# One hand-set order for the end of each attention layer and the start of the Fourier layer behind it

## The chip, the cores and the metric

The kernel runs on one NeuronCore of a Trainium2 chip. The core has five engines that each work through a queue of their own, in order: TensorE (PE in the profile) for matrix products, VectorE (DVE), ScalarE (ACT), GpSimd (POOL), and SyncE (SP), which here only issues transfers. ACT issues some transfers as well. The metric is the device time of one execution in microseconds (us), the median over runs.

## The reference

Four layers work on x, 2048 rows of 640 numbers. Layers 0 and 2 are attention with a sliding, dilated window of 8 keys and 32 heads of 20; layers 1 and 3 are Fourier mixing, a product with a 2048x2048 matrix from the left and with a 640x640 matrix from the right. All is float32.

```python
def _A_ref(x, wqkv, wo):
    qkv = (x @ wqkv).reshape(B, S, 3, H, Dh)...
    idx = pos[:, None] - off[None, :]          # off = 0, 2, .., 14
    logits = jnp.einsum("bhsd,bhswd->bhsw", q, kg) * scale   # masked where idx < 0
    o = jnp.einsum("bhsw,bhswd->bhsd", _softmax(logits), vg)
    return o.reshape(B, S, D) @ wo

def _B_ref(x, dft_seq_re, dft_seq_im, dft_hid_re, dft_hid_im):
    a = jnp.einsum("bsd,ed->bse", x, dft_hid_re)
    b = jnp.einsum("bsd,ed->bse", x, dft_hid_im)
    return jnp.einsum("ts,bse->bte", dft_seq_re, a) - jnp.einsum("ts,bse->bte", dft_seq_im, b)

x = x + _A_ref(_layernorm(x), A_wqkv, A_wo)
x = x + _B_ref(_layernorm(x), B_dft_seq_re, B_dft_seq_im, B_dft_hid_re, B_dft_hid_im)
x = x + _A_ref(_layernorm(x), A_wqkv, A_wo)
x = x + _B_ref(_layernorm(x), B_dft_seq_re, B_dft_seq_im, B_dft_hid_re, B_dft_hid_im)
```

## The kernel before

**Numbers in two parts.** Every operand of a large product is kept as a high part (a rounded copy, made by ACT) and a low part (what is left, made by DVE or POOL with a subtraction). A product is three passes: high by high, high by low, low by high. To "split" a tile means to make both parts. Line numbers below are those of the kernel before.

**Attention layer** (`layer_a`, layers 0 and 2). The rows are handled in four chunks of 512, each of four tiles of 128 rows. The work is spread over numbered steps; a table `plan` holds for each step and each of some 35 phases the operations that fall there, and the lists in `CFG['ly']` set step and phase of nearly everything (`wo`: output products, `ln`: normalisations for the next layer, `t2`, `t3`: transpositions of the last chunks, `kvq`: which stores ACT issues instead of SP, and so on; many entries are half a step or a phase). The whole runs under a manual schedule: each engine gets its instructions in exactly the order in which they are written.

**Fourier layer** (`LayerB`, layers 1 and 3). Its first product, for a tile t of the sequence matrix, sums 16 blocks in five PSUM banks, m0, m1, xt, t0 and t1: `z_mm(s, p, t)` (L1114) is block s, 15 matmuls of 128x512 (five banks, three passes), or a third of it. The blocks of the first tile (t = 0) are already worked off inside the attention layer as its chunks get done. A block needs its row tile, normalised and split, and its piece of the matrix: loaded by `c_load` or `cw_load`, its high part made by `c_hi` on ACT (L1065), its low part by `c_lo` on DVE (L1097). In layer 0, `c_put` stores both parts to memory, from where layer 2 fetches them.

**The end of an attention layer**, behind the last step, stands in program text in a fixed order: last transposition (`pc_pe(67)`, L438, into bank pq; `pc_hi` L442 on ACT, `pc_lo` L459 on DVE), the last two output products (`wo_mm`, L636), and for each of the last two row tiles `wo_add` (L254 on DVE, stored by `wo_store`, L653), `wo_stats` (L259 to L268 on ACT), `wo_fin` (L276, only where the 1/sqrt is POOL's), `ln_tail` (L1051 on ACT for the high part, L1052 on DVE for a normalised copy) and `ln_lo` (L1039). Between them stand the splits of blocks 14 and 15 (layer 0 only) and `z_mm` 14 and 15. `z_late` are thirds of earlier blocks that are put off to the end: one in layer 2 (`z_late(68)`), none in layer 0.

**The start of the Fourier layer** (`run`). `evac(0)` copies the five banks out as high parts (`zt_put`: ACT, L1165) and low parts (DVE, L1167 and L1170) into tiles zo0, zo1, zo2 and ot; the banks are then free for the second tile, whose blocks s = 0 to 15 follow: `cw_load`, split, `z_mm(s, None, 1)`. Around them stand, in numbers set by `pre` and `post` in `CFG['run']`, the splits of the weights of the second product (`load_w`: transfers L297 into the two buffers called xa, ACT L225, DVE L227 and L229), sums of input tiles (`x_whole` L1243, `x_combine` L1253 to L1256), and, at the blocks listed in `y`, pieces of the first tile's second product (`ymm`, L1188, 12 matmuls each).

In `run` only PE is under the manual schedule. A scheduler that works with modelled times puts the instructions of the other engines in order, and may move those of `run` ahead, between the last operations of the attention layer:

```python
        def run(self, nstats):
            ...
            self.evac(0)
            ...
            with tc.manual_schedule(engines={nc.tensor.engine}):
                for s in range(NST):
                    ...
                    self.zpart(1, s, s + 1)
```

In `Stats`, `lno` decides for each chunk whether 1/sqrt(variance) is two ACT operations (logarithm and exponential) or a power on POOL; `lnv` decides for each row tile whether DVE or POOL makes its low part.

Of the kernel before, what the change touches and what calls it, by code (L numbers as in the profile page):

```python
# [55 lines left out]
 'wqg': [0, 0, 0, 0, 0, 1, 0, 1, 1, 1, 0, 1, 0, 1, 1, 0, 1, 0, 1, 0],  # L56
 'run': [{'pre': [0, 1, 0, 0, 2, 0, 0, 1, 0, 0, 0, 3, 0, 0, 0, 0],
          'post': [5, 1, 1, 2, 3, 4, 0, 5, 0, 7, 0, 3, 0, 4, 1, 5],
          'y': [[4, 4, 5, 6, 6], [9, 13, 14, 15, 16]]},
         {'pre': [6, 1, 0, 2, 3, 3, 0, 3, 0, 6, 0, 0, 2, 0, 0, 0],  # L60
          'post': [0, 0, 3, 2, 0, 4, 0, 0, 1, 0, 1, 0, 4, 0, 4, 3],
# [5 lines left out]
         'ord': [[2, 0, 1, 3, 4, 6, 5, 7], [2, 0, 1, 4, 6, 5, 3, 7], [0, 2, 1, 4, 3, 6, 5, 7]],  # L67
         'out': [20, 23, 27, 32, 36, 40, 44, 46],
         'wo': [22, 22, 26, 26, 29, 30, 33, 34, 39, 39, 42, 42, 45, 47, 49, 49],
# [5 lines left out]
         'z': [148, 149, 149, 151, 151, 156, 157, 157, 159, 159, 161, 162, 167, 168, 170, 171, 171, 173, 174, 175,  # L75
               175, 175, 176, 177, 179, 180, 180, 180, 181, 186, 186, 187, 188, 188, 188, 190, 191, 193, 194, 198,
# [4 lines left out]
         't2': [48, 48, 48, 48, 52, 52, 52, 52],  # L81
         't3': [57, 58, 60, 60],
         'wst': [0, 0, 0, 0, 0, 0, 0, -1, 0, 0, 0, 0, -1, 1, 0, 0],
         'kvq': [1, 0, 0, 1, 0, 0, 1, 0, 0, 0, 0, 0, 1, 0, 0, 0, 0, 0, 0, 0, 0, 0, 1, 0, 0, 0, 1, 0, 1, 0, 1, 0],
# [5 lines left out]
         'ph': ['evac dma peT0 pe hi fin peL z0 z1 red0 pe2 qk dma2 sA sB red1 sC av0 loE sD sE exp actl evacA sF '  # L90
                'evacO av1 qc dmaw dmac actL pe3w misc clo lnl dmas dmar pe3',
                'peT0 evac dma hi z0 peL red0 pe pe2 z1 fin qk dma2 sA av0 sD sE sB red1 loE sC evacA actL sF evacO '
                'exp dmac av1 actl qc misc clo dmas lnl dmar dmaw pe3 pe3w'],
# [3 lines left out]
         'lno': [True, False, False, True],  # L97
         'whole': [7, 57, 61],
         'lnv': [1, 1, 1, 0, 0, 1, 0, 0, 0, 1, 0, 0, 1, 1, 1, 1],
# [7 lines left out]
         'wo': [23, 23, 26, 27, 30, 31, 34, 35, 38, 38, 42, 42, 46, 47, 48, 49],  # L107
         'woph': 'z1',
         'ln': [41, 42, 42, 46, 53, 54, 55, 55],
# [3 lines left out]
         'z': [148, 150, 151, 151, 151, 152, 155, 156, 159, 160, 162, 169, 169, 170, 170, 170, 171, 171, 174, 174,  # L113
               175, 175, 177, 178, 178, 179, 179, 181, 182, 185, 186, 186, 186, 186, 187, 187, 188, 189, 192, 193,
               199, 205],
         'early': [5.3, 2.4, 6.1, 8.4, 5.9, 6, 7.3, 8.8, 7.4, 9.3, 13, 13.6, 9.3],
         'ym': [-7, 0],
         'ymph': 'pe2',
         't2': [49, 49, 48, 48, 50, 52, 52, 52],
         't3': [59, 58, 60, 60],  # L120
         'wst': [0, 0, 0, 1, 0, 0, 0, 0, 0, 0, 0, 0, 0, 0, 0, 0],
         'kvq': [1, 1, 1, 0, 0, 0, 0, 0, 0, 0, 0, 0, 0, 1, 0, 0, 1, 0, 0, 0, 0, 0, 1, 0, 0, 0, 0, 0, 0, 0, 1, 0],
# [4 lines left out]
         'zla': [0, 0, 2, 0, 0, 0, 1, 0, 1, 0, 0, 1, 0, 2],  # L127
         'ph': ['peT0 dma evac hi red0 pe z0 peL qk z1 fin sA pe2 red1 dma2 sB sD sC av0 loE sE clo evacA exp actl '
                'actL sF evacO av1 qc dmaw dmas misc pe3 lnl dmar dmac pe3w',
                'peT0 evac pe z0 dma red0 hi fin peL pe2 sA z1 qk dma2 sB red1 av0 sD loE evacA sC sE exp actL evacO '  # L130
                'sF av1 dmas dmaw actl qc misc dmar lnl pe3w clo dmac pe3'],
# [33 lines left out]
def tile_layers(ctx: ExitStack, tc: tile.TileContext, x, wqkv, wo, cs, cst, wre, wim, out):  # L165
# [178 lines left out]
    def layer_a(li, stats, handoff, prev):  # L344
# [623 lines left out]
        with tc.manual_schedule(engines=ENGINES):  # L968
# [8 lines left out]
            busy("pc_pe 67")  # L977
            pc_pe(67)
            pc_hi(67)
            pc_lo(67, True)  # L980
            busy("wo_mm 3 2 3")
            wo_mm(c, 2, None, 0, 2, 3)
            z_late(67)
            busy("wo_mm 3 3")
            wo_mm(c, 3, ("pq", "aux0"))
            z_late(68)
            wo_add(c, 2)
            wo_stats(c, 2)
# [5 lines left out]
            handoff.ln_tail(c, 2, xr, nstats)
            wo_add(c, 3)
            handoff.ln_lo(c, 2)
            busy("z_mm 14")
# [4 lines left out]
            if first:  # L1002
                handoff.c_hl(15)
                if CFG["cput"][15]:
                    handoff.c_put(15)
# [548 lines left out]
```

## Time and profile before

| | |
|---|---|
| median of 3 runs | 1750.72 us (1750.36 to 1752.07) |
| profiled execution | 1751.65 us, span of its instructions 1749.9 us |
| matmuls | 8828 |
| busy | PE 1720.2, DVE 1357.8, ACT 821.6, POOL 617.7 us |
| granted clock of TensorE, mean | 0.999 |
| transfers | 419.91 MB, mean 240 GB/s |

The page gives the busy time of each engine, groups of instructions and the chain of waits. The timeline lists an engine's instructions in order: start, duration, engine, line, operation, tiles, shapes, how many were merged, and in brackets how long the engine had been idle before and whose end it waited for. In the names of tiles numbers are left out: "m" is m0 or m1, "t" is t0 or t1, "s" is any of s0 to s3, "r" the large weight and input tiles. Matmuls overlap, so a matmul's duration is longer than the distance to the next one. Layer 0 ends at about 384 us, layer 1 at about 865, layer 2 at about 1249.

### The profile page before, as it was taken

The page shows a single profiled execution, that of the slowest core. Times are in us where ns is not written, and L with a number is a line of the kernel's source. Part 1 is how long each engine was busy: PE and PEld are TensorE (multiplying, and loading weights), DVE is VectorE, ACT ScalarE, POOL GpSimd, SP SyncE. Part 2 cuts the span into 40 slices and gives each one's busy share as a digit, 9 for nine tenths or more (in the row PEclk, how much of TensorE's full clock was granted, in tenths as well). Part 3 has the DMA queues.
Part 4 walks back from the last instruction along what each step waited for, and adds up shares of the span by engine and source line. Part 5 has one row for each costly group of instructions (what it writes and reads, how often), then busy time and mean ns, then how long its engine had stood idle before and what let it go on. Part 6 is the DMA issues. An engine that isn't in the chain of part 4 may idle for free.

```text
span 1749.9 us, 26561 instructions
## 1 busy us (share of the span) xinstructions
PE 1720.2 (98%) x8828; PEld 1497.1 (86%) x8828; DVE 1357.8 (78%) x2117; ACT 821.6 (47%) x1814; POOL 617.7 (35%) x572
## 2 busy tenths in 40 slices
PE   9999999999999999999999999999999999999999
PEld 6888888778888888888888889888788888888888
DVE  5999999878767767767639998899786677677673
ACT  5654644654445445445534434445443443443441
POOL 4899999940000000000019997899200000000000
PEclk9999999999999999999999999999999999999999
DMA  6786668968787687687557865788697867867861
GB/s 235 246 295 198 206 229 309 338 212 317 250 263 228 215 271 232 210 276 224 188 163 256 280 201 182 236 300 287 205 356 227 263 205 253 263 217 237 262 205 53
DMA packets 266713, 419.91 MB, mean 240 GB/s; under 512 B 22192, under 2 KB 144560, under 8 KB 266320
## 3 DMA queue, kind: packets, MB, share of 16 engines
q1 hardware_dynamic: 255088, 410.68, 71.1%
q10 hardware_dynamic: 11488, 7.54, 1.4%
q8 instruction: 70, 1.15, 0.3%
q14 instruction: 67, 0.55, 0.1%
HBM read 332.99 MB, written 85.14 MB: 239 GB/s over the span
## 4 chain that ended last, share of the span: by engine, by line
PE 81%; DVE 6%; DMA 4%; POOL 3%; ACT 3%; issue 2%; SPq 0%; ACTq 0%; DVEq 0%; POOLq 0%
PE m L473 16%; PE aux L1188 15%; PE m L1289 11%; PE t L1289 10%; PE aux L636 6%; PE pq L1289 5%; PE xt L1289 5%; PE t L1114 4%; PE m L1114 4%; PE xt L1114 2%; DVE pr L553 2%; DVE pr L596 1%; POOL pr L611 1%; DMA win<-cs_in 1%; POOL pr L556 1%
## 5 line engine op out<-in xcount | busy, mean ns | idle before, releaser
L473 PE MATMUL m<-r,s 128*128 128x512 f32 (+1 forms) x1920 | 429.3, 379 | 1.5 <-DVE r L755 0.9
L473 PEld LDWEIGHTS m<-r,s 128*128 128x128 f32 x1920 | 350.3, 188 | 57.5 <-DVE r L755 1.3
L1282 ACT CAST r<-win 128x512 fp32r<-128x512 f32 x242 | 147.1, 620 | 174.5 <-DVE win L1318 104.2
L1188 PE MATMUL aux<-r2a,zo 128*128 128x320 f32 x768 | 226.0, 309 | 0.0
L553 DVE TENSOR_TENSOR pr<-pq,win 128x1280 f32<-128x1280 f32 x128 | 189.8, 1483 | 37.8 <-PE aux L1188 20.3
L611 POOL TENSOR_TENSOR pr<-pr 128x640 f32<-128x640 f32 x126 | 207.6, 1648 | 26.3 <-DVE pr L596 25.2
L556 POOL TENSOR_TENSOR pr<-pr 128x640 f32<-128x640 f32 x125 | 179.5, 1436 | 88.8 <-DVE pr L553 88.7
L1188 PE MATMUL aux<-pr,zo 128*128 128x320 f32 x704 | 208.0, 309 | 0.0
L1283 DVE TENSOR_TENSOR r<-win,r 128x512 fp32r<-128x512 f32 x242 | 162.7, 687 | 41.4 <-ACT r L1282 39.0
L596 DVE TENSOR_TENSOR pr<-pq,win 128x1280 f32<-128x1280 f32 x128 | 190.3, 1488 | 2.5
L276 POOL TENSOR_TENSOR stats<-stats,mhalf 128x1 f32<-128x1 f32 (+1 forms) x27 | 19.6, 725 | 468.7 <-ACT stats L270 468.7
L1289 PE MATMUL m<-r,r 128*128 128x512 f32 x600 | 153.2, 390 | 0.8 <-DVE r L1283 0.7
L1188 PEld LDWEIGHTS aux<-r2a,zo 128*128 128x128 f32 x768 | 144.1, 188 | 2.1
L1188 PEld LDWEIGHTS aux<-pr,zo 128*128 128x128 f32 x704 | 132.2, 188 | 2.4
L1289 PEld LDWEIGHTS m<-r,r 128*128 128x128 f32 x600 | 112.3, 188 | 24.6 <-DVE r L1283 1.6
L1289 PE MATMUL t<-r,r 128*128 128x512 f32 x492 | 131.9, 390 | 0.0
L612 POOL TENSOR_TENSOR pr<-pr 128x320 f32<-128x320 f32 x126 | 113.5, 901 | 9.9
L566 DVE TENSOR_REDUCE lg<-pr 128x64 f32<-128x640 f32 (+1 forms) x128 | 105.8, 827 | 12.7 <-POOL pr L556 12.5
L1318 DVE TENSOR_TENSOR win<-win,win 128x512 f32<-128x512 f32 x109 | 75.0, 690 | 48.9 <-DMA win<-cs_in 47.6
L1114 PE MATMUL m<-s,r 128*128 128x512 f32 x348 | 107.3, 395 | 4.1 <-DVE zo L1167 1.3
L1289 PEld LDWEIGHTS t<-r,r 128*128 128x128 f32 x492 | 92.3, 188 | 19.8
L1114 PE MATMUL t<-s,r 128*128 128x512 f32 x348 | 106.5, 394 | 2.7 <-DVE ot L1170 2.3
(296 smaller groups left out, 3236.0 us busy)
## 6 DMA issues: line engine op xcount, KB each, us to landing
win<-cs_in SPq DMA_DIRECT2D x346, 256.0 KB, 4.2
r<-xc SPq DMA_DIRECT2D x240, 256.0 KB, 4.2
win<-kvb SPq DMA_DIRECT2D x96, 440.0 KB, 4.6
xa<-cs_in SPq DMA_DIRECT2D x120, 256.0 KB, 4.1
win<-kvb SPq DMA_DIRECT2D x64, 360.0 KB, 5.2
xc<-sg SPq DMA_DIRECT2D x28, 512.0 KB, 5.6
xr<-xs SPq DMA_DIRECT2D x40, 320.0 KB, 3.7
kvb<-stg SPq DMA_DIRECT2D x36, 320.0 KB, 2.6
```

The lines of the kernel that those rows point to most:

```text
L473: nc.tensor.matmul(mt[g][:, : GW[q]], st[:, a, k], wq[q][:, b, k], start=n == 0, stop=n == 14)
L553: nc.vector.tensor_tensor(pr, q, wview(u, jp, 0, [[1, FE]]), op=ALU.mult)
L556: nc.gpsimd.tensor_tensor(pv[:, :, 0:10], pv[:, :, 0:10], pv[:, :, 10:20], op=ALU.add)
L566: nc.vector.tensor_reduce(rows(lgs[u], jp), pv.rearrange("p (a h) d -> p a h d", h=HE), axis=AX.X, op=ALU.add,)
L596: nc.vector.tensor_tensor(pr.rearrange("p j w (h d) -> p (j w) h d", d=DH), rows(lgs[u], jp).unsqueeze(3).to_broadcast([P, 2 * W, HE, DH]) ...
L611: g.tensor_tensor(pr[:, :, 0:4], pr[:, :, 0:4], pr[:, :, 4:8], op=ALU.add)
L612: g.tensor_tensor(pr[:, :, 0:2], pr[:, :, 0:2], pr[:, :, 2:4], op=ALU.add)
L1114: self.last = nc.tensor.matmul(self.z[t][k], self.xn[c][:, a, j, k * P : (k + 1) * P], self.ct[s][:, b], start=s == 0 and i == 0, stop=s = ...
L1188: self.last = nc.tensor.matmul(self.ym[e][:, :320], zt[(k, a, ri)][:, j2 * P : (j2 + 1) * P], w[:, e * 320 : (e + 1) * 320], start=(k, a, ...
L1282: nc.scalar.copy(hi, raw)
L1283: nc.vector.tensor_tensor(lo, raw, hi.bitcast(F32), op=ALU.subtract)
L1289: nc.tensor.matmul(bank, w(a, kb), hl[b], start=start and (a, b) == (0, 0), stop=stop and (a, b) == (1, 0),)
```

## The change

The end of the attention layer becomes a list of small operations, one letter each, and `CFG['ly'][..]['tail']` gives the order of all of them, for layer 0 and for layer 2. The list now also holds the eviction of the first tile, piece by piece (`E`, `e0` to `e4`), the loads of the second tile's first three blocks (`G0` to `G2`) and the splits of its first two (`h0 k0 h1 k1`: high and low part), all under the manual schedule of every engine. `run` does those of the first three that the list leaves out, and everything that it schedules itself is issued behind the last instructions of the eviction on ACT and DVE. In layer 0, the splits and stores of blocks 14 and 15 (`c14 d14 p14 c15 d15 p15`) come first; in layer 2 the put-off third (`z68`) does.

```diff
+         'tail': 'c14 d14 p14 c15 d15 p15 P H L M2 z67 M3 z68 A2 S2 F2 T2 A3 l2 Z14 z69 S3 F3 T3 l3 G0 G1 G2 Z15 E '
+                 'e0 h0 k0 e1 e2 e3 e4 h1 k1'},
...
+         'tail': 'z68 P H L M2 z67 M3 A2 S2 F2 c14 d14 p14 T2 A3 l2 Z14 z69 S3 F3 c15 d15 p15 T3 l3 G0 G1 G2 Z15 E '
+                 'e0 h0 k0 e1 e2 e3 e4 h1 k1'}],
...
-            wo_add(c, 2)
-            wo_stats(c, 2)
-            wo_fin(c, 2, 3)
-            if first:
-                handoff.c_hl(14)
...
+            done = C["tail"].split()
+            assert all(t[0] in "Ghk" for t in set(tail) - set(done))
+            for t in done:
+                tail[t]()
+            h.done = set(done)
...
-            self.evac(0)
...
-            with tc.manual_schedule(engines={nc.tensor.engine}):
+            with ExitStack() as st:
+                for x in (self.last_a, self.last_v):
+                    st.enter_context(tc.issue_after(x.ins))
+                st.enter_context(tc.manual_schedule(engines={nc.tensor.engine}))
                 for s in range(NST):
...
-                    self.zpart(1, s, s + 1)
+                    for t, fn in (("G", lambda: self.cw_load(1, s)), ("h", lambda: self.c_hi(s, 1)), ("k", lambda: self.c_lo(s))):
+                        if f"{t}{s}" not in self.done:
+                            fn()
+                    self.z_mm(s, None, 1)
```

Around this many entries of the tables move by a half-step, a step or a phase; three to name:

```diff
-         'lno': [True, False, False, True],
+         'lno': [True, False, False, False],
...
-         'lnv': [1, 1, 1, 0, 0, 1, 0, 0, 0, 1, 0, 0, 1, 1, 1, 1],
+         'lnv': [1, 1, 1, 0, 0, 1, 0, 0, 0, 1, 0, 0, 1, 1, 0, 1],
...
-          'y': [[4, 4, 5, 6, 6], [9, 13, 14, 15, 16]]},
+          'y': [[3, 4, 5, 6, 8], [9, 13, 14, 14, 15]]},
```

In layer 0 the last chunk's 1/sqrt thus goes to POOL, and so does the low part of the tile before the last; and the pieces of the second product stand behind blocks 3, 4, 5, 6 and 8 instead of 4, 4, 5, 6 and 6.

ACT at the end of layer 0, before, from the last tile's statistics on (`s` at L1065 are splits of blocks, `r2a` and `pr` at L225 weights, `zo` at L1165 the eviction):

```order
L267 ACTIVATE stats_3928<-stats_3928,eps_65 128x1
L268 ACTIVATE stats_3928<-stats_3928 128x1
L1065 CAST s_660_4257<-win_4117 128x512
L284 ACTIVATE stats_3928<-stats_3928 128x1
L1051 ACTIVATE r_3_636_4047<-xa_4142,stats_3928 128x640
L225 ACTIVATE pr_675_4331<-xa_4332 128x640
L1065 CAST s_667_4303<-win_4301 128x512
L1065 CAST s_684_4356<-win_4354 128x512
L1165 CAST zo_662_4282<-m_496_3155 128x512
L1165 CAST zo_662_4282<-m_497_3156 128x256
```

And in the changed kernel (whose line numbers are a little higher: L1074 for L1065, L1060 for L1051, L1164 for L1165, L229 for L225):

```order
L274 ACTIVATE stats_3935<-stats_3935 128x1
L288 ACTIVATE stats_3935<-stats_3935 128x1
L1060 ACTIVATE r_3_637_4048<-xa_4143,stats_3935 128x640
L1164 CAST zo_666_4288<-m_496_3155 128x512
L1074 CAST s_670_4294<-win_4267 128x512
L1164 CAST zo_666_4288<-m_497_3156 128x256
L1164 CAST zo_667_4289<-m_497_3156 128x256
L1164 CAST zo_667_4289<-xt_3157 128x512
L1164 CAST zo_668_4290<-t_499_3158 128x512
L1164 CAST ot_4291<-t_500_3159 128x512
L1074 CAST s_671_4308<-win_4269 128x512
L229 ACTIVATE r2a_4334<-xa_4335 128x640
```

The split of block 15 is gone from between the statistics and the normalisation, and no weight and only block 0's split stands ahead of or within the eviction.

DVE at the same place, before, from block 15's low part on (L1243 is a sum of input tiles):

```order
L1097 TENSOR_TENSOR s_660_4257<-win_4117,s_660_4257 128x512
L1052 TENSOR_SCALAR win_4261<-xa_4142,stats_3928 128x640
L1243 TENSOR_TENSOR s_695_4432<-r_2_569_3615 128x1024
L1039 TENSOR_TENSOR r_3_636_4047<-win_4261,r_3_636_4047 128x640
L227 SCALAR_TENSOR_TENSOR pr_675_4331<-xa_4332,pr_675_4331 128x640
L1097 TENSOR_TENSOR s_667_4303<-win_4301,s_667_4303 128x512
L1097 TENSOR_TENSOR s_684_4356<-win_4354,s_684_4356 128x512
L1167 TENSOR_TENSOR zo_662_4282<-m_496_3155,zo_662_4282 128x512
L1170 TENSOR_TENSOR zo_663_4283<-m_497_3156,zo_662_4282 128x256
L1170 TENSOR_TENSOR zo_663_4283<-m_497_3156,zo_663_4283 128x256
L1167 TENSOR_TENSOR zo_664_4284<-xt_3157,zo_663_4283 128x512
L1243 TENSOR_TENSOR s_696_4434<-r_0_418_2649 128x1024
```

And in the changed kernel (L1106 for L1097, L1061 for L1052, L1245 for L1243, L1048 for L1039, L1166 and L1169 for L1167 and L1170):

```order
L1061 TENSOR_SCALAR win_4262<-xa_4143,stats_3935 128x640
L1048 TENSOR_TENSOR r_3_637_4048<-win_4262,r_3_637_4048 128x640
L1166 TENSOR_TENSOR zo_666_4288<-m_496_3155,zo_666_4288 128x512
L1106 TENSOR_TENSOR s_670_4294<-win_4267,s_670_4294 128x512
L1169 TENSOR_TENSOR zo_667_4289<-m_497_3156,zo_666_4288 128x256
L1169 TENSOR_TENSOR zo_667_4289<-m_497_3156,zo_667_4289 128x256
L1166 TENSOR_TENSOR zo_668_4290<-xt_3157,zo_667_4289 128x512
L1169 TENSOR_TENSOR zo_668_4290<-t_499_3158,zo_668_4290 128x256
L1169 TENSOR_TENSOR ot_4291<-t_499_3158,zo_668_4290 128x256
L1166 TENSOR_TENSOR ot_4291<-t_500_3159,ot_4291 128x512
L1245 TENSOR_TENSOR s_698_4447<-r_2_570_3616 128x1024
L1245 TENSOR_TENSOR s_699_4449<-r_0_419_2651 128x1024
```

Both sums have moved from within the eviction to behind it; block 1's low part follows them.

PE at the end of layer 2, before (aux with r2a are output products, pq the last transposition, m the banks of the first product):

```order
L636 MATMUL aux_1798_12507<-r2a_9372,zo_1787_12455 128x320 x9
L438 MATMUL pq_12517<-ident_69,zo_1749_12175 128x128 x4
L636 MATMUL aux_1797_12497<-r2a_9372,zo_1787_12455 128x320 x6
L636 MATMUL aux_1798_12507<-r2a_9372,zo_1787_12455 128x320 x6
L636 MATMUL pq_12538<-r2a_9372,zo_1789_12457 128x320 x15
L636 MATMUL aux_1801_12554<-r2a_9372,zo_1789_12457 128x320 x15
L1114 MATMUL m_1658_11591<-s_1774_12336,r_3_1779_12392 128x512
```

And in the changed kernel:

```order
L640 MATMUL aux_1798_12505<-r2a_9373,zo_1787_12453 128x320 x9
L1123 MATMUL m_1659_11591<-s_1774_12338,r_3_1779_12385 128x512
L1123 MATMUL m_1660_11592<-s_1774_12338,r_3_1779_12385 128x512
L1123 MATMUL xt_11593<-s_1774_12338,r_3_1779_12385 128x512
L1123 MATMUL t_1662_11594<-s_1774_12338,r_3_1779_12385 128x512
L1123 MATMUL t_1663_11595<-s_1774_12338,r_3_1779_12385 128x512
L442 MATMUL pq_12520<-ident_69,zo_1750_12176 128x128 x4
L640 MATMUL aux_1797_12495<-r2a_9373,zo_1787_12453 128x320 x6
L640 MATMUL aux_1798_12505<-r2a_9373,zo_1787_12453 128x320 x6
```

The five matmuls of the put-off third have moved from behind the output products to ahead of the transposition.

More of the change, by code (lines that the diff above doesn't have):

```diff
@@ L994, in layer_a @@
[L994 to L997, printed above, removed]
-            handoff.z_mm(14, None)
-            z_late(69)
-            wo_stats(c, 3)
-            wo_fin(c, 3, 4)
[L1002 to L1005, printed above, removed]
-            handoff.ln_tail(c, 3, xr, nstats)
-            handoff.ln_lo(c, 3)
-            busy("z_mm 15")
-            handoff.z_mm(15, None)
+            none = lambda *a: None
@@ new lines, in layer_a @@
+            h = handoff
+            tail = {
+                "P": lambda: (busy("pc_pe 67"), pc_pe(67)),
+                "H": lambda: pc_hi(67),
+                "L": lambda: pc_lo(67, True),
+                "M2": lambda: (busy("wo_mm 3 2 3"), wo_mm(c, 2, None, 0, 2, 3)),
+                "M3": lambda: (busy("wo_mm 3 3"), wo_mm(c, 3, ("pq", "aux0"))),
+                "E": lambda: h.zt_new(0),
+            }
+            for j in (2, 3):
+                s = 12 + j
+                tail |= {
+                    f"A{j}": lambda j=j: wo_add(c, j),
+                    f"S{j}": lambda j=j: wo_stats(c, j),
+                    f"F{j}": lambda j=j: wo_fin(c, j, j + 1),
+                    f"T{j}": lambda j=j: h.ln_tail(c, j, xr, nstats),
+                    f"l{j}": lambda j=j: h.ln_lo(c, j),
+                    f"c{s}": (lambda s=s: h.c_hi(s)) if first else none,
+                    f"d{s}": (lambda s=s: h.c_lo(s)) if first else none,
+                    f"p{s}": (lambda s=s: h.c_put(s)) if first and CFG["cput"][s] else none,
+                    f"Z{s}": lambda s=s: (busy(f"z_mm {s}"), h.z_mm(s, None)),
+                }
@@ new lines, in layer_a @@
+            for t in (67, 68, 69):
+                tail[f"z{t}"] = lambda t=t: z_late(t)
+            for s in range(3):
+                tail |= {
+                    f"G{s}": lambda s=s: h.cw_load(1, s),
+                    f"h{s}": lambda s=s: h.c_hi(s, 1),
+                    f"k{s}": lambda s=s: h.c_lo(s),
+                }
+            for k in range(KD):
+                tail[f"e{k}"] = lambda k=k: h.evac1(0, k)
+            done = C["tail"].split()
+            assert all(t[0] in "Ghk" for t in set(tail) - set(done))
```

90 lines of the change are left out of this document (36 added, 54 removed), and 16 rows, old and new, of the table CFG.

## The prediction

> **What bounds the kernel now.** I read the page first, then busy time in stretches of 50 us, then the timeline of each engine around the two places where an attention layer hands over to a Fourier layer.
>
> ```profile
> PE 1720.2 (98%) x8828; PEld 1497.1 (86%) x8828; DVE 1357.8 (78%) x2117; ACT 821.6 (47%) x1814; POOL 617.7 (35%) x572
> 350.00:400.00 50.00, 45.38 (x222) 37.70 (x221) 39.20 (x66) 25.94 (x62) 18.30 (x17) 0.97 0.60 199
> ```
>
> TensorE (PE) is busy for 98% of the span, and the change leaves its matmuls the same in number and shape. So only PE's waits can be won or lost: 1749.9 - 1720.2 = 29.7 us of idle, and whatever hides in matmuls that ran slowly. The stretch 350 to 400 has the most idle of all (4.6 us) and a granted clock of 0.97. Inside it, PE (start, duration, last the idle before it and who ended it):
>
> ```profile
> 383.43 0.61 PE L1114 MATMUL t<-s,r 128*128 128x512 f32 x2
> 384.83 0.73 PE L1114 MATMUL m<-s,r 128*128 128x512 f32 x2 [0.78 <-ACT r L1051]
> 386.80 1.24 PE L1114 MATMUL m<-s,r 128*128 128x512 f32 x4 [1.24 <-DVE r L1039]
> ...
> 389.12 2.51 PE L1114 MATMUL t<-s,r 128*128 128x512 f32 x6
> 392.03 1.69 PE L1114 MATMUL m<-s,r 128*128 128x512 f32 x6 [0.40 <-DVE zo L1167]
> ...
> 395.92 1.63 PE L1114 MATMUL t<-s,r 128*128 128x512 f32 x6 [1.50 <-DVE ot L1170]
> 397.38 0.62 PE L1114 MATMUL m<-s,r 128*128 128x512 f32 x2
> ...
> 400.80 0.62 PE L1114 MATMUL m<-s,r 128*128 128x512 f32 x2
> ```
>
> From 397.38 to 400.80 one block of 15 matmuls takes 3.42 us, 0.228 each. Block 15 of the first tile could have begun at 383.43 + 2 x 0.228 = 383.89; it and block 0 of the second tile are over at 397.38. That is 13.49 us for 30 matmuls that need 6.84: **6.65 us lost**. Four of them are waits (0.78, 1.24, 0.40, 1.50), the rest is refilling after each and a slow stretch: six matmuls from 389.12 take 2.51, six from 392.03 take 1.69.
>
> Who was late is read from ACT, then DVE, then SP's queue:
>
> ```profile
> 373.64 0.65 ACT L442 CAST zo<-pq 128x256 fp32r<-128x256 f32 x2 [6.00 <-PE pq L438]
> ...
> 379.36 0.92 ACT L1051 ACTIVATE r<-xr,stats 128x640 fp32r<-128x640 f32 x1
> ...
> 382.59 0.29 ACT L267 ACTIVATE stats<-stats,eps 128x1 f32<-128x1 f32 x1
> ...
> 383.02 0.60 ACT L1065 CAST s<-win 128x512 fp32r<-128x512 f32 x1
> 383.53 0.29 ACT L284 ACTIVATE stats<-stats 128x1 f32<-128x1 f32 x1
> 383.86 0.92 ACT L1051 ACTIVATE r<-xa,stats 128x640 fp32r<-128x640 f32 x1
> 388.58 0.74 ACT L225 ACTIVATE pr<-xa 128x640 fp32r<-128x640 f32 x1 [3.80 <-DMA xa<-wim_in]
> ...
> 390.41 1.13 ACT L1165 CAST zo<-m 128x512 fp32r<-128x512 f32 x3
> ```
>
> ```profile
> 374.32 0.76 DVE L459 TENSOR_TENSOR zo<-pq,zo 128x256 fp32r<-128x256 f32 x2 [3.57 <-ACT zo L442]
> ...
> 384.79 1.22 DVE L1243 TENSOR_TENSOR s<-r 128x1024 f32<-128x1024 f32 x1
> 385.93 0.82 DVE L1039 TENSOR_TENSOR r<-win,r 128x640 fp32r<-128x640 f32 x1
> ...
> 391.30 0.68 DVE L1167 TENSOR_TENSOR zo<-m,zo 128x512 fp32r<-128x512 f32 x1
> ```
>
> ```profile
> 381.23 0.32 SPq L653 DMA_DIRECT2D xs<-xa  x1
> 382.70 0.33 SPq L297 DMA_DIRECT2D xa<-wim_in  x1
> ```
>
> Three things stand in the way. Block 15's own cast (L1065) is in ACT's queue ahead of the last tile's normalisation (L1051). A sum for later work (L1243, 1.22) is in DVE's queue ahead of that tile's low part (L1039), on which PE waits 1.24. And ACT stands 3.80 us at a weight that is still on its way (L225, issued 382.70, there at 388.58: 5.9 us), with the eviction's casts (L1165) queued behind it until 390.41, though bank m0 was complete by about 387.7. PE then waits for the eviction bank by bank.
>
> **The change part by part.** *Layer 0's hand-over.* The order shows that all three are taken away. Blocks 14 and 15 are split before the last transposition, where ACT is idle 6.00 and DVE 3.57 us: two casts and two subtractions, nothing on the path. The weight casts and sums stand behind the whole eviction. Against it, the last chunk's 1/sqrt now goes through POOL, and so does the low part of the tile before the last. POOL's groups (busy us, mean ns of one) and, from the page, the median landing of a block's data:
>
> ```profile
> L1039 POOL TENSOR_TENSOR r<-r,r 128x640 fp32r<-128x640 f32 x10 | 15.7, 1571 | 0.0
> L276 POOL TENSOR_TENSOR stats<-stats,mhalf 128x1 f32<-128x1 f32 x20 | 11.2, 562 | 11.8 <-ACT stats L270 11.8
> ```
>
> ```profile
> win<-cs_in SPq DMA_DIRECT2D x346, 256.0 KB, 4.2
> ```
>
> The moved low part starts when its high part is there, 379.36 + 0.92 and a little, say 380.4, and ends at 382.0; block 14 begins at 383.89 - 3.42 = 380.47 and wants it for its eleventh matmul, at 382.75, so it costs nothing.
>
> For the rest I keep the old times up to 382.59. One ACT operation of some 0.2 (L284, the nearest row, takes 0.29), POOL's 0.56 and two hand-overs of 0.05 (384.78 to 384.83) give 383.45; the bias 0.33 (383.53 to 383.86) and L1051's 0.92 give 384.70. PE begins at 384.75, **0.86** after it could. Nothing stands ahead of the low part on DVE now, so it follows at once: 384.75 + 0.82 = 385.57. PE has issued two matmuls until 385.21 and waits **0.41**. The other 13 end at 388.58. Bank m0 is complete at about 386.0; ACT's cast (0.62 by L1065's kind) and DVE's subtraction (0.68) free it at 387.35, block 0's cast follows on ACT at once and its subtraction is done by 387.95, before 388.58. DVE's other four pieces are 0.6 to 0.7 each and end by 390.5; PE reaches the last bank at 388.58 + 12 x 0.228 = 391.3. So the eviction is hidden, by 0.6 to 0.8 us; were that cover gone, each late piece would show as the 0.40 and 1.50 do now. Block 0's transfer is now issued straight behind the store at 381.23; at the median 4.2 it lands at 385.8, at the 5.9 seen above at 387.5, and then costs about 0.2. Next late is block 1: behind the eviction DVE has two sums (L1243) before block 1's subtraction: 390.5 + 2 x 1.15 + 0.7 = 393.5, where block 1 (from 392.0) wants it for its sixth matmul at 393.14: **0.36**. Loss 0.86 + 0.41 + 0.36 = 1.63 for 6.65: **-5.0 us**.
>
> This counts PE at its full clock. Before, a half-rate stretch followed 2.9 us (383.89 to 386.80) of which 2.02, 70%, was waiting; now 1.27 of the same length is, 44%, and I take no drop. [...]
>
> *Layer 2's hand-over*, PE and one row of ACT:
>
> ```profile
> 1244.28 0.62 PE L1114 MATMUL m<-s,r 128*128 128x512 f32 x2
> ...
> 1248.85 1.56 PE L1114 MATMUL m<-s,r 128*128 128x512 f32 x6
> ...
> 1253.34 0.97 PE L1114 MATMUL m<-s,r 128*128 128x512 f32 x3 [0.88 <-DVE zo L1167]
> ...
> 1259.19 0.62 PE L1114 MATMUL m<-s,r 128*128 128x512 f32 x2
> ```
>
> ```profile
> 1247.29 0.92 ACT L1051 ACTIVATE r<-xa,stats 128x640 fp32r<-128x640 f32 x1
> ```
>
> 1248.85 to 1259.19 is 10.34 for 6.84: 3.50 lost, and block 15 itself did not wait: the first wait (0.88) is for the eviction, as are the others. Now it will. Five matmuls move from behind the last output product (which ends at 1244.28) to ahead of the last transposition, so only block 14's 3.42 us cover the chain to L1051's end, 1248.21 - 1244.28 = 3.93. That is 0.5 of wait, less about 0.05 for a weight cast that leaves ACT's queue; then 0.41 and 0.36 as above: 1.2 for 3.50, **-2.3 us**.
>
> *Half-steps.* They move single operations in ACT's, DVE's, PE's and SP's queues. Between 110 and 270 us and inside the Fourier layers PE hardly waits, and I cost them at nothing there: the cover is PE's own queue of ready matmuls. Six transfer issues in layer 0 and three in layer 2 go from SP to ACT, which is busy for only 47%. One weight split at the start goes from POOL to DVE; its weights are wanted only after 60 matmuls. What counts is at the ends of the attention layers, where PE waits at present:
>
> ```profile
> 289.90 0.39 PE L446 MATMUL aux<-ot,nident 128*128 128x256 f32 x1 [1.21 <-ACT s L442]
> ...
> 348.20 0.49 PE L446 MATMUL aux<-s,nident 128*128 128x512 f32 x1 [0.68 <-ACT s L442]
> 349.38 4.66 PE L636 MATMUL aux<-r2a,s 128*128 128x320 f32 x30 [0.68 <-ACT s L461]
> ...
> 1153.09 0.33 PE L438 MATMUL aux<-ident,zo 128*128 128x128 f32 x1 [0.53 <-POOL zo L613]
> ...
> 1201.04 0.44 PE L446 MATMUL aux<-ot,nident 128*128 128x384 f32 x1 [1.09 <-ACT ot L442]
> ...
> 1207.20 0.39 PE L446 MATMUL aux<-ot,nident 128*128 128x256 f32 x1 [0.73 <-ACT s L442]
> ```
>
> In layer 0 five matmuls (5 x 0.228 = 1.14) now stand ahead of the first and the third of these: 1.1 and 0.68 less. Elsewhere a transposition and its subtraction now follow each other directly, which waits 0.68 as in the second row; a transposition comes sooner behind the product in the same bank, and block 12 may wait for its tile, whose 1/sqrt stands in POOL's queue behind the attention sums. I take 0.4 for each, between 0 and the 1.2 of the first row. Sum **-0.3**, between -1.8 and +1.3. In layer 2 the last three go (a normalisation that blocked ACT moves a step earlier, and five matmuls go between), 2.35 less, and one pair of the 0.68 kind is new: **-1.7**, between -2.4 and 0, since other waits may take their place.
>
> **Sum.** -5.0 - 2.3 - 0.3 - 1.7 = -9.3. The profiled execution took 1751.65 (span 1749.9, and 1.75 around it that stays), so 1742.35; the median of the runs is 1750.72, 0.93 below it: **1741.4 us**.
>
> **The rivals.** *The clock falls again (0.10).* For it: the window row's 0.97 and the slow six matmuls. Against it: the 44% above. If it comes, six matmuls cost 0.82 more, as at 389.12, and some 12 of them fill such a stretch: 1.7, so 1743.1.
>
> *The half-steps give it back (0.06).* For it: the new pairs above. Against it: no wait of this kind in the profile exceeds 1.21. Four more of 1 us make -9.3 + 4 = -5.3, and a block 0 that lands 1.3 later than 387.5 in both layers, 1.1 net each, -3.1: 1747.6, no change that shows.
>
> *The weights come late, and it is slower (0.05).* The ten weight loads share two buffers and are now split only behind the eviction, the first by about 394. A pair takes landing 5.9 + cast 0.74 + subtraction 0.82 = 7.5 us. The fourth piece of the second tile's product stands behind block 6 and three pieces of 12 matmuls (0.15 each, 30 in 4.66 above): 392.4 + 6 x 3.42 + 3 x 1.8 = 418.3, and its pair is there at 394 + 3 x 7.5 = 416.5. From 6.5 us of landing on PE waits, and ACT and DVE have the next block's splits queued behind the load. At 9 us it costs 3 x 2.5 = 7.5 in each layer, +15 - 9.3: 1756.4. Against it: blocks' data land in 4.2 at the median.
>
> **How the numbers follow.** The forecast has 0.79, the rivals the rest. Its own ends: all bounds on the good side (-5.0 - 2.3 - 1.8 - 2.4) and some refilling saved behind each wait that goes, near 1736.5; the half-steps at nothing and transfers late, near 1747. That range, **1736.5 to 1747**, holds the clock rival too. A measurement of this kernel can tell about 0.2%, 3.5 us, from no change: faster 0.91, same 0.04, slower 0.05.
>
> **What would show it.** Right: no ACT wait for a weight ahead of the eviction's casts; block 15 preceded by waits near 0.9 and 0.4 in both layers; no wait of PE on zo or ot; granted clock 1.00 in that stretch; 30 matmuls in 8 to 8.5 us. Wrong: PE waiting on zo, on pieces of block 1 or 2 for over 1 us, on a weight at the second product, or new waits above 1.2 between 270 and 350 or 1140 and 1230 us.

## The result, and the profile after

| | before | changed |
|---|---|---|
| median of runs | 1750.36 us (6 runs) | 1742.82 us (6 runs, 1740.89 to 1745.26) |
| profiled execution | 1751.65 us, span 1749.9 | 1743.01 us, span 1741.2 |
| granted clock, mean | 0.999 | 1.000 |

The ratio is 0.9958, with a 95% interval of 0.9946 to 0.9971: 7.4 us faster, where 9.3 were forecast. Below, a gain over the kernel before is worked out from such a ratio, unless it is said to be by the medians. The forecast of 1741.4 was 1.4 us too low and its range held the result. Of the 1.4, 0.7 is the sum (the profiled executions are 8.6 apart, not 9.3), and 0.7 is the step from the profiled execution to the median: the forecast took 0.93 off, as before, and the changed kernel's median is only 0.2 below its profiled execution.

The page of the changed kernel, and its window of 350 to 400 us (PE, PEld, DVE, ACT, POOL busy, then the granted clock):

```profile
PE 1717.2 (99%) x8828; PEld 1496.2 (86%) x8828; DVE 1360.1 (78%) x2117; ACT 822.6 (47%) x1810; POOL 616.1 (35%) x574
350.00:400.00 50.00, 47.58 (x239) 39.83 (x239) 39.86 (x67) 25.27 (x58) 20.79 (x20) 1.00 0.61 207
```

Idle time of PE is 1741.2 - 1717.2 = 24.0 us, before 29.7; the other 3.0 us of the 8.7 come off PE's busy time itself. Up to 1.7 of them is the half-rate stretch (387.80 to 391.21 at a granted clock of 0.50, last section); the rest was not followed up. In the stretch of the hand-over 2.4 us of idle are left of 4.6, at a clock of 1.00 instead of 0.97. The same stretch of layer 0 on PE, ACT and DVE (start, duration; in brackets the idle time before and its end):

```profile
383.70 0.61 PE L1123 MATMUL t<-s,r 128*128 128x512 f32 x2
384.91 2.05 PE L1123 MATMUL m<-s,r 128*128 128x512 f32 x6 [0.59 <-ACT r L1060]
...
392.25 0.62 PE L1123 MATMUL m<-s,r 128*128 128x512 f32 x2
...
392.93 0.61 PE L1123 MATMUL t<-s,r 128*128 128x512 f32 x2
393.66 0.73 PE L1123 MATMUL m<-s,r 128*128 128x512 f32 x2
```

```profile
383.61 0.29 ACT L288 ACTIVATE stats<-stats 128x1 f32<-128x1 f32 x1 [0.66 <-POOL stats L280]
...
386.30 0.59 ACT L1164 CAST zo<-m 128x512 fp32r<-128x512 f32 x1 [1.45 <-PE m L1123]
...
390.05 0.74 ACT L229 ACTIVATE r2a<-xa 128x640 fp32r<-128x640 f32 x1
```

```profile
384.89 0.82 DVE L1048 TENSOR_TENSOR r<-win,r 128x640 fp32r<-128x640 f32 x1 [0.67 <-ACT r L1060]
...
390.65 2.35 DVE L1245 TENSOR_TENSOR s<-r 128x1024 f32<-128x1024 f32 x2
392.91 0.69 DVE L1106 TENSOR_TENSOR s<-win,s 128x512 fp32r<-128x512 f32 x1
```

Block 15 could begin at 383.70 + 2 x 0.228 = 384.16 and block 1 begins at 392.25: 8.09 us for 30 matmuls (before 13.49). That is 1.25 lost, and 0.27 in front of block 1's sixth matmul (392.93 + 0.46 = 393.39, to 393.66), behind the two sums: 1.52 for 6.65. Term by term it is 0.75 (forecast 0.86), 0.50 (0.41) and 0.27 (0.36). No wait for zo or ot is left. ACT's eviction now waits for PE (1.45 for bank m0), no longer PE for the eviction, and the weight stands behind it at 390.05.

PE at the hand-over of layer 2:

```profile
1241.98 0.61 PE L1123 MATMUL t<-s,r 128*128 128x512 f32 x2
1242.89 2.05 PE L1123 MATMUL m<-s,r 128*128 128x512 f32 x6 [0.29 <-ACT r L1060]
...
1250.22 0.62 PE L1123 MATMUL m<-s,r 128*128 128x512 f32 x2
```

Block 15 could begin at 1241.98 + 2 x 0.228 = 1242.44 and begins 0.45 later. Block 1 begins at 1250.22, 7.78 us for 30 matmuls (before 10.34), and loses 0.28 more behind the sums: 1.22 in all for 3.50.

Where the rest went is read from three marks that both programs have: the last subtraction on PE in layer 0 (L446, a product with a negative identity, behind the transposition before the last), the transposition for layer 2 that waits 0.92 for DVE (others stand ahead of it), and the last subtraction on PE in layer 2; of before, then changed, then a second profile of the changed kernel (run e8 below):

```profile
366.30 0.82 PE L446 MATMUL aux<-zo,nident 128*128 128x384 f32 x2 [0.24 <-ACT zo L442]
855.56 0.44 PE L327 MATMUL pq<-ident,xa 128*128 128x128 f32 x2 [0.92 <-DVE s L338]
1232.37 0.82 PE L446 MATMUL aux<-zo,nident 128*128 128x384 f32 x2 [0.24 <-ACT zo L442]
```

```profile
366.54 0.83 PE L450 MATMUL aux<-zo,nident 128*128 128x384 f32 x2 [0.52 <-ACT zo L446]
850.07 0.44 PE L331 MATMUL pq<-ident,xa 128*128 128x128 f32 x2 [0.92 <-DVE s L342]
1225.93 0.82 PE L450 MATMUL aux<-zo,nident 128*128 128x384 f32 x2 [0.24 <-ACT zo L446]
```

```profile
365.60 0.82 PE L450 MATMUL aux<-zo,nident 128*128 128x384 f32 x2 [0.47 <-ACT zo L446]
848.58 0.44 PE L331 MATMUL pq<-ident,xa 128*128 128x128 f32 x2 [0.92 <-DVE s L342]
1223.53 0.82 PE L450 MATMUL aux<-zo,nident 128*128 128x384 f32 x2 [0.24 <-ACT zo L446]
```

| stretch | forecast | changed | changed, second profile |
|---|---|---|---|
| start to the first mark (half-steps) | -0.3 | +0.24 | -0.70 |
| first to second mark (hand-over, layer 1) | -5.0 | -5.73 | -6.28 |
| second to third mark (half-steps) | -1.7 | -0.95 | -1.86 |
| the rest (hand-over, layer 3; spans 1741.2, 1738.2) | -2.3 | -2.26 | -2.86 |

Two profiles of one program differ by 0.5 to 1 us in each row, so the rows bear out the forecast's sizes for the two hand-overs and agree with those of the half-steps only roughly. The second profile is of the shortest of its six runs. Single waits of under 1 us should not be read from one profile alone.

### The profile page after: what moved, and what is told of

Same layout as the page of the kernel before. It is cut to its first block, busy times and chain, and to the rows that moved or that the text cites. A ratio compares the mean times of both kernels' runs of the same rounds, so it can differ in the third digit from the quotient of the medians.

```text
span 1741.2 us, 26545 instructions
## 1 busy us (share of the span) xinstructions
PE 1717.2 (99%) x8828; PEld 1496.2 (86%) x8828; DVE 1360.1 (78%) x2117; ACT 822.6 (47%) x1810; POOL 616.1 (35%) x574
```

## The experiments

**e1: the hand-over alone.** All tables of before, with the new list at the layers' ends.

```diff
  CFG of before, and in it:
+         'tail': ... (both lists of the change)
-         'lno': [True, False, False, True],  'lnv': [..., 1, 1, 1, 1],
+         'lno': [True, False, False, False], 'lnv': [..., 1, 1, 0, 1],
```

> The kernel before with nothing but the new order of the layer's end (both hand-set lists, the sums and weights behind the eviction, the last chunk's 1/sqrt and one low part on POOL); all other tables, also those of the Fourier layer's start, stay as before. Theory (the gain is the hand-over's): 30 matmuls of layer 0's hand-over in about 8.5 us, of layer 2's in about 8.1, together -7.3. But the first product's pieces stand behind blocks 4, 4, 5, 6 and 6 here. In the trace of the changed kernel the fifth weight of the second kind is cast at 422.08 + 0.74 and its low part takes 0.82 more, 423.7; here the fifth piece would begin at about 420.0 (block 0 begins 388.7, seven blocks of 3.42, four pieces of 1.8 and 0.1 of change). So a wait of 2.5 to 4 in layer 1 in front of the fifth piece: net -3.3 to -4.8, about 1746.3. Rival (the weights have cover enough): no wait there, -7.3, 1743.1. Rival (half-steps carry the gain): hand-overs come out at -4 or less, 1748 or more.

Measured: 1750.01 us, ratio 0.9997 (0.9988 to 1.0006): no gain at all. The hand-overs are as short as in the changed kernel (the wait for L1060 is 0.59 again). PE and, below it, ACT of this run in layer 1, and the window around them:

```profile
419.92 0.31 PE L1190 MATMUL aux<-r2a,ot 128*128 128x320 f32 x1
423.19 0.63 PE L1190 MATMUL aux<-zo,ot 128*128 128x320 f32 x1 [2.97 <-ACT zo L229]
...
426.52 0.63 PE L1123 MATMUL m<-s,r 128*128 128x512 f32 x2
```

```profile
422.41 0.74 ACT L229 ACTIVATE zo<-xa 128x640 fp32r<-128x640 f32 x1 [0.17 <-DMA xa<-wim_in]
...
420.00:430.00 10.00, 7.03 (x29) 5.82 (x28) 8.78 (x14) 4.83 (x10) 0.00 (x0) 0.83 0.96 355
```

The fifth piece waits 2.97 for the last weight, as the theory had it (2.5 to 4). What the theory lacked is the price behind it: the next 11 matmuls take 426.52 - 423.19 = 3.33 instead of 1.6, at a granted clock of 0.83 in that window. So the late weight costs 3.1 + 1.7 = 4.8 instead of 3.5. Another wait of 1.73, at the start of a pair of tiles in layer 1, takes some more in this profile; e2 and e3 show waits of that kind too. From the first mark to the second this profile takes 489.9 us, before 489.3: what layer 0's hand-over gains is lost again in layer 1. The mean clock of each of the 11 runs is 0.997 to 0.999.

**e2: the hand-over with the pieces' table.**

```diff
  e1, and:
-          'y': [[4, 4, 5, 6, 6], [9, 13, 14, 15, 16]]},
+          'y': [[3, 4, 5, 6, 8], [9, 13, 14, 14, 15]]},
  ('pre', 'post' and layer 3's row likewise as in the change)
```

> The one before this, with the changed kernel's table for the Fourier layer's start as well (pieces of the second product behind blocks 3, 4, 5, 6 and 8; weights and sums between the blocks as there). Theory: no wait on a weight, so the hand-overs' whole -7.3: 1743.1, within 1 us of the changed kernel, and the half-steps together are worth next to nothing. Rival (half-steps carry 2 us, as the forecast had it): 1743.1 here and the changed kernel 2 us below it. Rival (weights late in spite of it): PE waits in front of a piece, over 1745.

Measured: 1743.90 us, ratio 0.9964 (0.9950 to 0.9978), so -6.3. No wait on a weight. Against e1, on the same chip and by the medians, this one table (places of the pieces, weights and sums) is worth 6.1 us. It makes the hand-over's gain, forecast at -7.3, nearly whole; in this profile waits of 0.93 and 1.07 stand at the starts of two pairs in layer 1, where the changed kernel's profile has none.

**e3: the half-steps alone.** The changed kernel's tables with the old order of the end, the old eviction and the old `lno`, `lnv`.

```diff
  CFG of the change, and in both layers:
-         'tail': 'c14 d14 p14 ... e4 h1 k1'
+         'tail': 'P H L M2 z67 M3 z68 A2 S2 F2 c14 d14 p14 T2 A3 l2 Z14 z69 S3 F3 c15 d15 p15 T3 l3 Z15'
+  self.evac(0) at the start of run, and no bound there
```

> The changed kernel's tables, but the layer's end and the eviction in the old order and under the scheduler, 1/sqrt and low parts as before. Theory by the trace of the changed kernel: waits between 270 and 381 us come out 0.3 worse, those between 1140 and 1240 about 0.9 better, so -0.6 in all and both hand-overs as long as before (13.5 and 10.3 us for 30 matmuls), with the half-rate stretch back in layer 0: 1749.8, same. The forecast had -2.0 for them: 1748.4. Rival (they carry the gain): 1746 or less.

Measured: 1747.80 us, ratio 0.9988 (0.9979 to 0.9997): -2.1. The forecast's -2.0 is borne out, and my later reading of -0.6, from one profile of the changed kernel, was too pessimistic. The hand-over is the old one, slow stretch included (six matmuls take 2.18, the next six 1.69; the mean clock of this profile is 0.999):

```profile
388.10 2.18 PE L1121 MATMUL t<-s,r 128*128 128x512 f32 x6
```

-6.3 of e2 and -2.1 of e3 make -8.4, beside -7.4 and -8.1 for the whole change (first runs and e8): the two parts add up.

**e4: weights and sums free to go ahead of the eviction.**

```diff
-                for x in (self.last_a, self.last_v):
-                    st.enter_context(tc.issue_after(x.ins))
```

> The changed kernel, but what the Fourier layer's start schedules itself may again be put ahead of the eviction on ACT and DVE (the two bounds that hold it behind are left out); everything else, the hand-set list too, stays. Here one weight's cast and two sums go ahead of the eviction again. Theory (it is the order of ACT's and DVE's queues that pays): sums (1.22 each) ahead of the low part and ACT standing at a weight bring back 1.2 to 2.5 in layer 0 and 1 to 2 in layer 2, with waits on the eviction's tiles: 1745.5 to 1747.5. If waiting again fills 70% of some 3 us, the granted clock falls in layer 0. Rival (early splits and stores alone pay): 1743.

Measured: 1749.33 us, ratio 0.9991 (0.9982 to 1.0000). Most of the gain is gone without these two lines of the program. ACT of this run stands at a weight in the middle of the eviction, and PE waits for bank xt:

```profile
389.00 0.74 ACT L230 ACTIVATE r2a<-xa 128x640 fp32r<-128x640 f32 x1 [1.12 <-DMA xa<-wre_in]
```

```profile
383.02 0.61 PE L1124 MATMUL t<-s,r 128*128 128x512 f32 x2
...
392.48 0.93 PE L1124 MATMUL xt<-s,r 128*128 128x512 f32 x3 [2.18 <-DVE zo L1167]
...
394.64 0.62 PE L1124 MATMUL m<-s,r 128*128 128x512 f32 x2
```

From 383.02 + 0.46 = 383.48 to 394.64 the 30 matmuls lose 4.32: 2.80 of layer 0's 5.13 are given back. Layer 2, read in the same way, loses 3.75, no less than before (3.50).

The median is 1.8 us above the upper end of what was expected, and the runs show what goes with it. Four of its 11 runs have a mean granted clock of 1.000 and take 1745.5 to 1747.9 (the profiled one is among them, with a granted clock of 1.00 from 380 to 400, behind the 2.18 too); the other seven, at 0.996 to 0.999, take 1749.0 to 1751.7. The means of the two groups are 3.7 us apart. The waits of the profile cost 0.3 and 0.5 more than the upper ends expected (2.5 and 2); the rest goes with the clock, though the runs without a trace do not show where it fell.

**e5 and e9: covering what is left.** The same kernel, on two chips.

```diff
  layer 0:
-         'z': [..., 198, 198, 199],
+         'z': [..., 198, 198, 205],
-  e4 h1 k1
+  h1 k1 e4
  layer 2:
-  z68 P H L M2 z67 M3 A2 ...  e4 h1 k1
+  P H L M2 z67 M3 z68 A2 ...  h1 k1 e4
```

> The changed kernel with the three remaining waits of each hand-over attacked by order alone: in layer 0 the last third of block 13 (five matmuls, 1.14 us) is put off to behind the last output product (as in layer 2 before), in layer 2 the put-off third goes back there, and in both layers block 1's split stands ahead of the eviction's last bank, so ahead of the two sums. Theory: the waits are what is left of the chain product, sums, statistics, power, normalisation, and 1.14 more of matmuls cover them: 0.75 and 0.30 go in layer 0, 0.46 and 0.30 in layer 2, 0.28 for block 1 in both: -2.4 against the changed kernel, about 1740.4, the 30 matmuls in about 6.9 us. Rival (the matmuls are missed where they are taken away): a wait of about 1 us appears in front of the last product or the last transposition, near 366 to 375 and 1225 to 1235, and the time stays at 1742.8. Rival (the last bank is late): a wait on ot of 0.5 or so in block 0.

Measured: 1741.92 us, ratio 0.9936 (0.9922 to 0.9950). Its profiled execution, 1745.20, was the longest of the five, with slow stretches at 12 to 20 us and at 330 to 335 us (granted clock 0.73 from 10 to 15, 0.59 from 15 to 20, 0.68 from 330 to 335). Hence e8 and e9, side by side:

> The changed kernel as it is, for comparison with the next two on the same chip: 0.996 of before. Its profile is a second look at what one profiled execution can't tell. Theory: the hand-overs come out as in the first profile (waits of 0.59 and 0.29 for the normalisation, 0.12 twice), since their length is set by the order of the queues; the waits that end with a transfer (1.69 at 325.94) and those at the starts of pairs in the Fourier layers (0 to 1.7 in the profiles so far) differ by up to 1 us. Rival: the hand-overs differ too.

> The kernel of e5 again, beside the changed kernel on the same chip. Theory: -2.4 against it (0.9986), and a profile without the two slow stretches at 12 to 20 and 330 to 335 us, since nothing of the edit lies there. Rival: the slow stretch at 330 belongs to this kernel (its wait for a transposed block's data is 0.2 longer), then it is there again, and the two kernels tie.

Measured: the changed kernel 1743.21 us, 0.9954 (0.9940 to 0.9969); this one 1741.57 us, 0.9944 (0.9929 to 0.9960). PE of e9 across blocks 14, 15, 0 and 1, without a wait, 30 matmuls from 382.98 to 389.98, 7.0 us:

```profile
382.98 1.68 PE L1123 MATMUL m<-s,r 128*128 128x512 f32 x6
...
389.98 0.62 PE L1123 MATMUL m<-s,r 128*128 128x512 f32 x2
```

The waits are gone, so they were the uncovered end of the chain. The profiles are 2.2 apart (spans 1738.2 and 1736.0), not 2.4, though e9 also waited 0.4 less at the transposition near 325 us (0.85, where e8 waits 1.26): some 0.8 came back in layer 1, where the eviction of the second tile is late:

```profile
461.82 0.94 PE L1291 MATMUL t<-r 128*128 128x512 f32 x3 [0.85 <-DVE ot L1169]
```

The slow stretches of e5 did not recur in this one further profile (mean clock 1.000, in e5's 0.997), so they are no fixed part of this kernel. By the medians the gain is 1.6 us, and the intervals of e8 and e9 overlap: likely, not shown.

**e6: one half-step of layer 2 undone.** PE's longest wait in the changed kernel's layer 2, and ACT's queue there:

```profile
1156.88 0.50 PE L450 MATMUL aux<-r,nident 128*128 128x256 f32 x2 [1.57 <-ACT r L446]
...
1163.92 1.30 PE L640 MATMUL aux<-r2a,s 128*128 128x320 f32 x7 [0.98 <-DVE r L258]
```

```profile
1154.44 0.43 ACT L530 COPY pq<-qs 128x320 f32<-128x320 f32 x1 [3.24 <-DVE pr L600]
1154.81 0.20 ACT L263 ACTIVATE stats<-stats 128x2 f32<-128x2 f32 x1
...
1156.20 0.63 ACT L446 CAST r<-aux 128x256 fp32r<-128x256 f32 x2
```

```diff
  layer 2, later steps:
-  ... dmas dmaw qc actl dmar lnl misc ...
+  ... dmas dmaw actl qc dmar lnl misc ...
```

> The changed kernel with one half-step of layer 2 undone: in its late steps the statistics of an output product stand ahead of the copy for the attention products again (one swap of two phases), as before. In the trace of the changed kernel PE waits 1.57 at 1156.88 for two casts on ACT, behind such statistics (1.6 us), which stand behind a copy that waits 3.24 for DVE. Theory: that order makes the wait; the statistics now run while ACT waits for DVE, the casts follow the copy at once, and the wait falls from 1.57 to 0.3 or so; nothing else is late: -1.2. Rival (the copy was moved forward for a reason): a copy behind statistics comes up to 1.6 later in other steps, DVE's attention products with it, and waits that the change took away come back (about 1 us at a transposition near 1200): +0.5 against the changed kernel.

Measured: 1742.92 us, ratio 0.9948 (0.9935 to 0.9960). PE of this run:

```profile
1154.73 0.50 PE L450 MATMUL aux<-r,nident 128*128 128x256 f32 x2 [0.74 <-ACT r L446]
...
1162.63 1.59 PE L640 MATMUL aux<-r2a,s 128*128 128x320 f32 x9 [1.83 <-DVE r L258]
...
1195.14 0.44 PE L450 MATMUL aux<-ot,nident 128*128 128x384 f32 x1 [1.05 <-ACT ot L446]
```

The wait falls by 0.8, the next one grows by 0.85, and the one that the change had taken away (1.09 at 1201.04 before) is back. The second profile of the changed kernel has 1.18 and 0.97 at the first two places, so the order explains about 0.4 to 0.8 of the first wait and not the 1.3 expected. The rival is right at these places; the times cannot tell the two apart.

**e7: blocks 14 and 15 split late again.**

```diff
-  c14 d14 p14 c15 d15 p15 P H L M2 z67 M3 z68 A2 S2 F2 T2 A3 l2 Z14 z69 S3 F3 T3 ...
+  P H L M2 z67 M3 z68 A2 S2 F2 c14 d14 p14 T2 A3 l2 Z14 z69 S3 F3 c15 d15 p15 T3 ...
```

> The changed kernel with the splits and stores of blocks 14 and 15 of layer 0 back in their old places (behind the statistics of the last two tiles); all else stays. The forecast named block 15's cast in ACT's queue as one of three things in the way. Theory 1 (the cast is in the way): with 1/sqrt on POOL, ACT stands idle 0.66 between the statistics and the bias, and the cast takes 0.62: it costs 0.0 to 0.1. Theory 2 (the store in SP's queue is in the way): the loads of the second tile's first blocks stand behind block 15's store, which now waits for its subtraction (about 384.3); block 0's data then land some 4.2 later, 388.9 or so, its split is done by 390.2, the eviction's pieces wait behind that split on ACT and DVE, and PE waits 1.5 to 2.5 in blocks 0 and 1: about 1744.8.

Measured: 1745.09 us, ratio 0.9960 (0.9947 to 0.9972). ACT of this run; SP's queue (L1145 loads the second tile's blocks), first of the changed kernel, then of this run; then PE of this run:

```profile
382.80 0.60 ACT L1074 CAST s<-win 128x512 fp32r<-128x512 f32 x1
...
388.20 0.62 ACT L1074 CAST s<-win 128x512 fp32r<-128x512 f32 x1 [1.36 <-DMA win<-cs_in]
```

```profile
381.83 1.39 SPq L1145 DMA_DIRECT2D win<-cs_in  x3
```

```profile
384.16 0.32 SPq L1077 DMA_DIRECT2D c0b<-s  x1
384.52 1.80 SPq L1145 DMA_DIRECT2D win<-cs_in  x3
```

```profile
384.86 2.04 PE L1123 MATMUL m<-s,r 128*128 128x512 f32 x6 [0.59 <-ACT r L1060]
...
389.60 1.69 PE L1123 MATMUL m<-s,r 128*128 128x512 f32 x5 [0.23 <-DVE s L1106]
...
394.99 0.73 PE L1123 MATMUL m<-s,r 128*128 128x512 f32 x2 [0.50 <-DVE s L1106]
```

Block 15's wait is 0.59 as ever: the cast fits into ACT's idle 0.66 and costs nothing. The loads are issued 2.69 later, behind the store, and blocks 0 and 1 begin to wait for their splits. This is theory 2. Summed over blocks 15 to 1 (384.11, where block 15 could begin, to 394.99, less the 35 matmuls of 7.98), 2.90 is lost instead of 1.52: 1.4, just under what was expected. This rests on the profiles; the ratio, 0.9960, cannot be told from the changed kernel's (0.9958, 0.9954).

**e10: the best one.** e9, with blocks 4 and 9 of layer 0 loaded instead of transposed on PE.

```diff
-         'cpe': [0, 0, 2, 0, 1, 0, 0, 0, 1, 2, 2, 0, 2, 0],
+         'cpe': [0, 0, 2, 0, 0, 0, 0, 0, 1, 0, 2, 0, 2, 0],
```

> The kernel of e5 with two blocks of layer 0 (4 and 9) loaded and split like most others instead of being transposed on PE from the transposed matrix; this takes eight transpositions off PE, and the pair of transposition and subtraction that now follow each other directly (0.68 at 334.95) and the one at 304.72 to 307.44 with it. Theory: each such pair was a wait of 0.84 with its refilling, and four transpositions of 0.1 go as well: -2 to -2.5 against e9, about 1738. Rival (one more transfer of 256 KB each crowds the queues): the data of a neighbouring block come late, a wait of 1 to 2 us for a transfer, no gain.

Measured: 1739.73 us, ratio 0.9936 (0.9923 to 0.9949), the fastest here, by the medians 3.5 below e8 and 1.8 below e9 on the same chip; the intervals overlap. The pair at 334.95 is gone. But the profile is not shorter than that of e9 (1737.5 against 1736.0); a product now waits for DVE:

```profile
312.38 4.67 PE L640 MATMUL aux<-r2a,r 128*128 128x320 f32 x30 [1.70 <-DVE r L258]
```

Why the medians fall and the profiles don't was not followed up.

## Why the prediction was right, and where its reasons were not

**Layer 0's hand-over, -5.0.** Right, and for the reason given: 6.65 became 1.52 (forecast 1.63). e4 shows that the weights and sums behind the eviction carry more than half of it: with them ahead again, 2.80 of the 5.13 come back. Of the three things that stood in the way, one is worth nothing here: block 15's cast does not hold up the normalisation's end once 1/sqrt is on POOL (e7). What its early place buys is SP's queue, where the store no longer holds up the next loads. The prediction had the moved issue nearly right (381.23, measured 381.83) but did not price it as a gain.

**The clock.** No drop was assumed, since PE waits for a smaller share of the time, and none came. In the worst 3.41 us (the length of the slow stretch before) of layer 0's hand-over PE is idle for 59% before (from 384.04) and for 21% in the changed kernel (from 384.32); from 380 to 400 the granted clock is 0.91 before and 1.00 in the changed kernel. That the share of waiting decides was the author's estimate from one slow stretch, and e4 does not bear it out (last section). The changed kernel's clock is 1.00 from 380 to 400 and from 1240 to 1260, the mean of its second profile is 1.000, and 9 of its 12 runs have a mean clock of 1.000, where 7 of the 47 runs of the kernel before that stand beside the experiments have. The rival's price was about right: no run shows its 12 slow matmuls, but e1 shows 11 behind one long wait, and 1.7 us.

**Layer 2's hand-over, -2.3.** Right. In the changed kernel block 15 waits 0.29 for L1060 and begins 0.45 late, as costed, and the loss of 1.22 is the 1.2 of the sum. e5 and e9 show that the five matmuls moved ahead of the last transposition were the missing cover, as the prediction had it.

**The half-steps, -2.0.** The sum is right (e3: -2.1), its terms less so. Gone are the three waits of layer 2 that were to go, or nearly (0.53 is 0.25). But the new pair there, costed at 0.68, waits 1.57 (1.18 in e8), since statistics and a copy stand in ACT's queue ahead of it (e6: they account for a part); and a wait of 0.98 for a sum, at 1163.92, was not foreseen. The 1.57 is one of the prediction's own signs of being wrong, a new wait above 1.2. That the sum came out is partly luck: terms missed in both directions.

**Inside the Fourier layers, nothing.** This was the weak step. The new places of the pieces were used in the sum for the weights (418.3 against 416.5) and not named as a part that has to be there. e1 shows that they are: with the old places the late-weights rival comes true, 4.8 us of wait and clock in layer 1, and the whole hand-over pays nothing. The prediction checked only the fourth piece, with a margin of 1.8 us. By its own terms the fifth, in its old place, would start at 418.3 + 1.8 = 420.1 and its pair be there at 416.5 + 7.5 = 424.0: a deficit.

## What to carry to other kernels

Work that is held back from a crowded hand-over is late somewhere else: follow it to whoever wants it next and move that, too, or the gain is lost again. Price a late step by the queue that it blocks, the issuing queue included, not by its own duration; a cast in an idle slot cost nothing, the store behind it 1.4 us. What waited at these hand-overs was the uncovered end of a chain, and independent matmuls that could be put off covered it (e9).

## What the runs showed of the hardware

The granted clock fell behind some waits and not behind others of about the same length. Rows of before, then the same place of the changed kernel (length, PE's busy time; third from the end the granted clock):

```profile
384.39:387.80 3.41, 1.73 (x6) 1.16 (x7) 2.35 (x3) 0.39 (x1) 0.00 (x0) 1.00 0.94 240
387.80:391.21 3.41, 3.41 (x9) 2.64 (x8) 1.86 (x3) 2.57 (x6) 0.00 (x0) 0.50 1.05 401
```

```profile
384.32:387.73 3.41, 2.69 (x11) 1.93 (x12) 1.63 (x3) 1.97 (x5) 0.00 (x0) 1.00 0.97 328
387.73:391.14 3.41, 3.41 (x17) 2.83 (x16) 3.41 (x8) 3.32 (x7) 0.00 (x0) 1.00 0.64 223
```

Before, PE was busy for 1.73 of 3.41 us, and the clock was 0.50 in the 3.41 us behind; in the changed kernel it was busy for 2.69, and the clock stayed at 1.00. Rows of e5, around a wait of 1.92 (326.93 to 328.85), then of e4, around one of 2.18 (390.30 to 392.48):

```profile
325.00:330.00 5.00, 3.08 (x18) 2.47 (x17) 3.55 (x4) 4.39 (x12) 4.84 (x6) 0.97 0.92 314
330.00:335.00 5.00, 5.00 (x17) 3.94 (x17) 4.93 (x5) 1.88 (x6) 4.92 (x5) 0.68 1.00 364
```

```profile
380.00:400.00 20.00, 16.50 (x71) 12.68 (x70) 17.08 (x28) 12.84 (x26) 1.98 (x2) 1.00 0.69 224
```

The longer wait is the one without a fall, so its length alone does not tell. Nor does the share of busy time, taken where PE waits most: in e4 the 3.41 us from 390.28 have only 1.23 of it, less than the 1.73 of before. What decides was not shown, nor what parts e4's two groups of runs.

Behind the wait of 2.97 in e1 the clock was 0.83 from 420 to 430, and 11 matmuls took 1.7 us longer than at full clock. For a forecast that is a price and not a rule: a long wait may cost some 1.7 us beside itself, an estimate from e1, and e4 has runs of one kernel with a mean clock of 1.000 and others at 0.996 to 0.999, 3.7 us apart.
